# A mixture-of-experts kernel with seven-product block multiplication: preparation steps held back during one product, one subtraction moved to GpSimd

## The chip, the core and the metric

The kernel runs on one core of one Trainium2 chip. The metric is the device time of one execution, in microseconds (us). In the texts below the engines have the names of the profile: PE is TensorE (matrix multiplication), DVE is VectorE, ACT is ScalarE, POOL is GpSimd, SP is SyncE, which issues the transfers.

## What is computed

Three layers follow each other, all in float32: an attention over short windows, a layer of four experts, and a feed-forward layer.

```python
# attention: 2 x 8 heads, 768 positions of 64; chunks of 32 see 16 to the left, 8 to the right and 8 memory keys
scores = scale * np.matmul(q_c, k_full.transpose(0, 1, 3, 2))
a = np.exp(scores - np.max(scores, axis=-1, keepdims=True)); a = a / (a.sum(-1, keepdims=True) + 1e-9)
out[:, :, c_start:c_end] = np.matmul(a, v_full)
# experts: x is 1536 x 512, four of them, hidden size 1024
p = domain_probs / (domain_probs.sum(-1, keepdims=True) + 1e-09)
for e in range(4):
    out += p[:, e:e + 1] * (np.maximum(x @ w1[e], 0.0) @ w2[e])
# feed-forward: hidden size 2048
h = x @ w_in
g = np.maximum(h, 0.0) + alpha * np.minimum(h, 0.0)
return g @ w_out
```

The weights of the last layer arrive as 64-bit floats and are turned into 32-bit ones on the chip.

## The kernel before, in words

**Tiling.** The hidden units of both layers are cut into 24 pairs of blocks, numbered p: 16 for the experts (p = 0 to 15) and 8 for the feed-forward layer (p = 16 to 23). The 1536 tokens are folded into 768 columns, and a tile is one p with 384 of these columns (c0 = 0 or 384). For a tile, `gemm1` (L654) multiplies the first weights by the tokens and applies the activation, and `gemm2` (or `gemm2_two`, `gemm2_rows`) multiplies the result by the second weights. PE's order is written out by hand in `order`: `gemm1` of a tile, then `gemm2` of the tile before. Around the change of layers two tiles are taken together: `gemm1` of p = 14 and 15 with the same columns and then one double `gemm2` for both, and the same for p = 16 and 17.

**Seven products.** `gemm1` computes a 2 x 2 block product with seven multiplications in place of eight: a, b, d, a again, c, d again, c again, in this order. The second parts of a, d and c accumulate on top of what is in the bank. Between the products DVE and ACT form sums: `add("c", t, q["b"])` (L738, in the trace `b<-c,t`) reads bank c after its first part, and the second part of c may start only when this reading is done. Its cover is the second part of d, six matmuls.

**Three passes.** Each float32 operand is split into a high part, a cast to the format that PE takes (ACT), and a low part, the rest (POOL or DVE). A product is high x high, high x low and low x high. So the activation leaves a `gg` tile in two steps of `high()` (L700): ACT's cast, then POOL's subtraction. `gemm2` needs both: for each block its third matmul reads POOL's low part.

**Preparation streams.** What prepares later work is written as generators: `w` (weights: combinations `s`, high parts `wh`, low parts `wl`), `c` (conversion of the 64-bit weights) and, between the layers, `x0` and `x384` (`transition`, which runs `prep_x` on three blocks of 128 columns each). Each `yield` gives the time at which the next step is due. The planner keeps a clock `now`, which moves by 0.013 + n/2400 us for each matmul of n columns, so by 0.173 us for 384. `product` (L647) is called for each matmul; before it traces the matmul, it traces every step that is due: `att_poll`, `begin`, `lag_poll` (activations) and `prep_poll` (the streams). Each engine then executes its instructions in exactly this program order (`keep_in_program_order`); semaphores alone tie the engines together. So what the planner decides is the order on each engine, not the time.

**prep_x (L164).** For a block of tokens it forms differences in a tile `st` of three slices. The pool of `st` has one buffer, which all blocks share. The order is: DVE writes slices 0, 1 and 2; then for z = 0 ACT casts slices 0 and 1 into `xh`, and DVE writes their low part into `xl` (L190); then DVE overwrites slice 1 with `b21 - st[:, 1]` (L184); then for z = 1 ACT casts slices 1 and 2, and DVE writes their low part. POOL writes the low parts of the plain tokens (L178, L188). The steps of `x0` are 1.1 us apart, those of `x384` 0.88 us.

**Names in the trace.** The helper that records instructions hides their lines (nearly all have L61), so the rows are read by tiles: `y` is a bank of `gemm2`, `st`, `xh`, `xl` belong to `prep_x`, `g` and `gg` to the activation, `wl` and `wh` to the weights, `u` and `t` to the sums.

Of the kernel before, what the change touches and what calls it, by code (L numbers as in the profile page):

```python
# [10 lines left out]
F32 = mybir.dt.float32  # L11
# [55 lines left out]
def tile_kernel(ctx: ExitStack, tc: tile.TileContext, qk, v, wa, wq, dpt, alpha, out):  # L67
    nc = tc.nc
    scale = 1.0 / float(D) ** 0.5
    pe_, dve, act, pool, sync = (Pinned(tc, e) for e in (nc.tensor, nc.vector, nc.scalar, nc.gpsimd, nc.sync))  # L70
# [71 lines left out]
    xh = xp.tile([P, 14, NCOL], F32R, name="xh")  # L142
    xl = xp.tile([P, 14, NCOL], F32R, name="xl")
# [5 lines left out]
    def acc_of(cs):  # L149
        h, c = divmod(cs.start, half)  # L150
        return acc[:, h, :, :, c:c + cs.stop - cs.start]
# [12 lines left out]
    def prep_x(c0, n):  # L164
        cs = slice(c0, c0 + n)
        here = acc_of(cs)
        b11, b12, b21, b22 = here[:, 0:2, 0], here[:, 0:2, 1], here[:, 2:4, 0], here[:, 2:4, 1]

        st = bp.tile([P, 3, 2, n], F32, tag="st", name=f"st{c0}")
        sub = ALU.subtract  # L170
        act.copy(xh[:, 0:4, cs], here[:, :, 0])
        dve.tensor_tensor(out=st[:, 0], in0=b12, in1=b11, op=sub)
        yield
        dve.tensor_tensor(out=st[:, 1], in0=b22, in1=st[:, 0], op=sub)
        act.copy(xh[:, 4:6, cs], b22)
        yield
        dve.tensor_tensor(out=st[:, 2], in0=b22, in1=b12, op=sub)
        pool.tensor_tensor(out=xl[:, 0:4, cs], in0=here[:, :, 0], in1=xh[:, 0:4, cs].bitcast(F32), op=sub)  # L178
        yield
        for z in (0, 1):  # L180
            r = slice(6 + 4 * z, 10 + 4 * z)
            t_ = st[:, z:z + 2].rearrange("p a b n -> p (a b) n")
            if z == 1:
                dve.tensor_tensor(out=st[:, 1], in0=b21, in1=st[:, 1], op=sub)  # L184
                yield
            act.copy(xh[:, r, cs], t_)
            if z == 0:
                pool.tensor_tensor(out=xl[:, 4:6, cs], in0=b22, in1=xh[:, 4:6, cs].bitcast(F32), op=sub)  # L188
            yield
            dve.tensor_tensor(out=xl[:, r, cs], in0=t_, in1=xh[:, r, cs].bitcast(F32), op=sub)  # L190
            yield

    def transition(c0, n):
# [149 lines left out]
    def att_poll(force=False):  # L343

        while True:
            due = [x for x in att["live"] if x[0] <= now[0] and clear(x[2])]
            room = att["next"] < NU and len(att["live"]) < LIVE and clear(att["next"])
            if due:
                x = due[0]
                try:  # L350
                    att["stage"][x[2]] += 1
                    lat = next(x[1])
                    x[0] = now[0] + lat
                except StopIteration:
                    att["live"].remove(x)
                    att["over"].add(x[2])
                    while att["done"] in att["over"]:
                        att["done"] += 1
            elif room and att["start"] <= now[0]:
                g = unit(att["next"])  # L360
                att["start"] = now[0] + (PACE0 if force else PACE)
                att["next"] += 1
                x = [0.0, g, att["next"] - 1]
                att["live"].append(x)
                x[0] = next(g) + now[0]
                att["stage"][x[2]] = 1
            elif force:
                times = [x[0] for x in att["live"] if clear(x[2])]
                if room:
                    times.append(att["start"])  # L370
                now[0] = max(now[0], min(times))
                continue
            else:
                return
            if force:
                return
# [228 lines left out]
    def step(name):  # L605
        x = streams[name]
        if x[1] is not None and not x[1]():
            return False
        try:
            x[0], x[1] = next(x[2])  # L610
        except StopIteration:
            del streams[name]
        return True

    def prep_poll():
        for name in list(streams):
            while name in streams and streams[name][0] <= now[0] and step(name):
                pass
# [15 lines left out]

    glist = []
    lag = []
    hold = [False]

    def later(t, f):
        lag.append((now[0] + t, f))  # L640
        lag.sort(key=lambda x: x[0])
# [5 lines left out]
    def product(*a, n, **kw):  # L647
        att_poll()
        begin()
        lag_poll()  # L650
        prep_poll()
        mm(*a, n=n, **kw)

    def gemm1(p, c0, n, parity, last):  # L654
        cs = slice(c0, c0 + n)
        nm = f"{p}_{c0}"
        q = {}

        def prod(z, a, b, start, stop):
            if start:  # L660
                q[z] = bank(f"{z}{nm}")[:, :n]
            prep_force("w", lambda: (p, a) in w1)
            while p == 0 and b >= T4 and att["x"] < -(-(c0 + n) // BLK):
                att_poll(force=True)
            wh, wl = w1[p, a]
            k = 0
            for kd in range(2):
                f = slice(kd * P, (kd + 1) * P)
                for w_, x_ in ((wh, xh), (wh, xl), (wl, xh)):
                    product(q[z], w_[:, f], x_[:, 2 * b + kd, cs], n=n,  # L670
                            start=start and k == 0, stop=stop and k == 5, skip_group_check=True)
                    k += 1
            if last:
                used1.add((p, USE.index(a)))

        def add(z, other, out):
            dve.tensor_tensor(out=out, in0=q[z], in1=other, op=ALU.add)

        def tmp(name):
            return bp.tile([P, 384], F32, tag=name, name=f"{name}{nm}")[:, :n]  # L680

        gs = {}

        def gelu(blk, src):

            i, ab = divmod(blk, 2)

            lag_poll(lambda: len(glist) < 2 or glist[-2][1] in glist[-2][0])
            glist.append((gs, blk))
            if p >= NP1 and i == 0:  # L690
                if ab == 0:
                    g2 = bp.tile([P, 2, 384], F32, tag="pb", bufs=2, name=f"g2_{nm}")
                    gs["g2"] = g2
                g = gs["g2"][:, ab, :n]
            else:
                g = bp.tile([P, 384], F32, tag="g", bufs=4, name=f"g{blk}_{nm}")[:, :n]
            gg = bp.tile([P, 2, 384], F32R, tag="gg" + "AB"[parity], bufs=4, name=f"gg{blk}_{nm}")
            gh, gl = gg[:, 0, :n], gg[:, 1, :n]

            def high():  # L700
                act.copy(gh, g)
                pool.tensor_tensor(out=gl, in0=g, in1=gh.bitcast(F32), op=ALU.subtract)
                gs[blk] = (gh, gl)

            def whole():
                dve.scalar_tensor_tensor(out=g, in0=src, scalar=0.0, in1=g,
                                         op0=ALU.max, op1=ALU.add)
                later(0.8, high)

            if p < NP1:  # L710
                pb = pb_t[2 * p * P // F1, c0, n]
                dve.scalar_tensor_tensor(out=g, in0=src, scalar=0.0, in1=pb[:, ab, :n],
                                         op0=ALU.max, op1=ALU.mult)
                later(0.7, high)
            else:
                fi = 2 * (p - NP1) + i

                def negative():
                    act.activation(g, src, AF.Relu, scale=-1.0)
                    act.mul(g, g, nalpha[:, fi:fi + 1])  # L720
                    later(1.4, whole)

                later(0.0, negative)

        hold[0] = p >= NP1
        prod("a", A11, B11, True, False)
        u2 = tmp("u2")
        act.copy(u2, q["a"])
        hold[0] = False
        prod("b", S2, T2, True, True)  # L730
        add("b", u2, u2)
        prod("d", S1, T1, True, False)
        t = tmp("t")
        add("d", u2, t)
        prod("a", A12, B21, False, True)
        gelu(0, q["a"])
        prod("c", S3, T3, True, False)
        add("c", t, q["b"])  # L738
        prod("d", S4, B22, False, True)
        gelu(3, q["b"])  # L740
        add("d", u2, q["d"])
        prod("c", A22, T4, False, True)
        gelu(1, q["d"])
        add("c", u2, q["c"])
        gelu(2, q["c"])
        return gs
# [187 lines left out]
    def begin():  # L934
        while begun and att["next"] >= begun[0][0]:
            begun.pop(0)[1]()

    for i, (what, k, *other) in enumerate(order):
        p, c0, n = tiles[k]
# [141 lines left out]
```

## Time and profile before

| what | value |
|---|---|
| time, median of 3 runs (lowest to highest) | 818.88 us (818.68 to 819.94) |
| time of the profiled execution | 816.98 us |
| its span from first to last instruction | 815.2 us |
| PE busy | 800.1 us, 98% of the span |
| DVE, POOL, ACT busy | 578.6, 563.2 and 330.8 us |

The span is the time from the first instruction to the last; 1.8 us of the profiled execution lie around it. The profiled execution is 1.9 us shorter than the median. Busy shares are means over the whole span; what a stage is bound by is read from the waits and from the engines' instructions in order of time.

### The profile page before, as it was taken

What the parts mean: (1) busy time and instruction counts of PE and PEld (TensorE: products, weight loads), DVE (VectorE), ACT (ScalarE), POOL (GpSimd) and SP (SyncE); (2) the same over time, 40 slices, a digit from 0 to 9 for tenths busy, and PEclk for the clock granted to TensorE, in tenths of its full rate; (3) what the DMA queues carried; (4) which work ended last, traced back from release to release, by engine and by line L of the source; (5) the groups of instructions that cost most, each with busy time, mean ns of one, the idle gap of its engine ahead of it and who ended that gap; (6) DMA issues with size and microseconds to landing.
All of it is one profiled execution on the core that took longest, in us unless ns stands there. A gap on an engine that the chain in (4) does not pass through costs nothing.

```text
span 815.2 us, 14396 instructions
## 1 busy us (share of the span) xinstructions
PE 800.1 (98%) x5439; PEld 763.3 (94%) x5439; DVE 578.6 (71%) x1087; ACT 330.8 (41%) x718; POOL 563.2 (69%) x587
## 2 busy tenths in 40 slices
PE   7989999999999999999999999999999999999998
PEld 5778999999999999999999999999798998998996
DVE  4777477867867877867877767587964877756555
ACT  3656524133223223323322323154762666555441
POOL 2867777777887877977787872293954987867511
PEclk9999999999999999999999999999999999999999
DMA  8792121332231332313422302001002132211003
GB/s 258 232 293 88 52 91 39 113 122 64 94 104 63 115 116 68 103 68 90 117 92 90 117 27 78 26 27 53 27 14 101 41 118 89 80 40 51 1 1 154
DMA packets 29781, 71.66 MB, mean 88 GB/s; under 512 B 4624, under 2 KB 7696, under 8 KB 29712
## 3 DMA queue, kind: packets, MB, share of 16 engines
q1 hardware_dynamic: 29712, 70.75, 26.3%
q8 instruction: 42, 0.69, 0.3%
q14 instruction: 27, 0.22, 0.1%
HBM read 59.18 MB, written 11.56 MB: 87 GB/s over the span
## 4 chain that ended last, share of the span: by engine, by line
PE 91%; DVE 3%; ACT 2%; DMA 2%; issue 1%; POOL 1%; SPq 0%; DVEq 0%; POOLq 0%; ACTq 0%
PE y L61 49%; PE a L61 12%; PE c L61 12%; PE d L61 11%; PE b L61 6%; DMA raw<-in_wa 1%; DMA qk<-in_qk 1%; PE x L61 1%; PE two L61 1%; DVE pe L61 1%; PE wps0.0_84 L61 0%; DVE mx L61 0%; SPq L61 0%; ACT pe L61 0%; ACT g L61 0%
## 5 line engine op out<-in xcount | busy, mean ns | idle before, releaser
L61 POOL TENSOR_TENSOR gg<-g,gg 128x384 fp32r<-128x384 f32 x192 | 202.2, 1064 | 118.9 <-ACT gg L61 116.9
L61 PE MATMUL y<-gg,wh 128*128 128x384 f32 x1024 | 265.1, 334 | 0.4 <-POOL gg L61 0.2
L61 DVE TENSOR_TENSOR acc<-y,acc 128x384 f32<-128x384 f32 (+1 forms) x296 | 170.1, 584 | 70.9 <-PE y L61 69.3
L61 PEld LDWEIGHTS y<-gg,wh 128*128 128x128 f32 x1024 | 185.1, 188 | 1.1 <-POOL gg L61 0.5
L61 PE MATMUL y<-gg,wl 128*128 128x384 f32 x512 | 171.1, 334 | 0.0
L61 ACT CAST gg<-g 128x384 fp32r<-128x384 f32 x192 | 97.6, 512 | 151.9 <-DVE g L61 151.5
L61 POOL TENSOR_TENSOR wl<-raw,wh 128x256 fp32r<-128x256 f32 (+1 forms) x112 | 114.1, 1027 | 44.5 <-ACT wh L61 28.7
L61 PE MATMUL y<-wh,gg 128*128 128x512 f32 x384 | 120.7, 390 | 0.0
L61 ACT COPY u<-a 128x384 f32<-128x384 f32 x48 | 23.0, 479 | 197.8 <-PE a L61 197.8
L61 PEld LDWEIGHTS y<-gg,wl 128*128 128x128 f32 x512 | 96.1, 188 | 0.0
L61 PEld LDWEIGHTS y<-wh,gg 128*128 128x128 f32 x384 | 72.0, 188 | 15.0 <-POOL gg L61 0.3
L61 PE MATMUL y<-wl,gg 128*128 128x512 f32 x192 | 74.9, 390 | 0.0
L61 POOL TENSOR_TENSOR wl<-s,wh 128x256 fp32r<-128x256 f32 x88 | 68.2, 782 | 4.4 <-ACT wh L61 4.1
L61 DVE TENSOR_TENSOR u<-b,u 128x384 f32<-128x384 f32 x48 | 26.8, 557 | 60.2 <-PE b L61 55.0
L61 POOL TENSOR_TENSOR fl<-fl,fm 128x512 f32<-128x512 f32 x32 | 41.3, 1292 | 32.8 <-DVE fm L61 20.7
L61 PE MATMUL a<-xh,wh 128*128 128x384 f32 x184 | 61.7, 335 | 0.0
L61 PE MATMUL a<-xh,wl 128*128 128x384 f32 x184 | 61.6, 335 | 0.0
L61 PE MATMUL d<-xh,wl 128*128 128x384 f32 x184 | 61.6, 335 | 0.0
L61 PE MATMUL d<-xl,wh 128*128 128x384 f32 x184 | 61.6, 335 | 0.0
L61 PE MATMUL a<-xl,wh 128*128 128x384 f32 x184 | 61.6, 335 | 0.0
L61 ACT CAST wh<-raw 128x256 fp32r<-128x256 f32 (+1 forms) x116 | 54.7, 492 | 16.8 <-PE y L61 14.2
L61 PE MATMUL d<-xh,wh 128*128 128x384 f32 x184 | 61.5, 334 | 0.0
(121 smaller groups left out, 1573.1 us busy)
## 6 DMA issues: line engine op xcount, KB each, us to landing
fr<-in_wq SPq DMA_DIRECT2D x32, 512.0 KB, 3.8
raw<-in_wa SPq DMA_DIRECT2D x28, 512.0 KB, 3.9
w2s<-fl SPq DMA_DIRECT2D x32, 256.0 KB, 2.4
raw<-w2s SPq DMA_DIRECT2D x16, 512.0 KB, 3.6
qk<-in_qk SPq DMA_DIRECT2D x24, 312.0 KB, 4.7
v<-in_v SPq DMA_DIRECT2D x48, 130.0 KB, 3.8
out<-acc SPq DMA_DIRECT2D x12, 256.0 KB, 2.0
pb<-p_dram SPq DMA_DIRECT2D x6, 384.0 KB, 3.5
```

The lines of the kernel that those rows point to most:

```text
L61: return self.tc.keep_in_program_order(f(*a, **kw))
```

## The change

While the first part of product c of a tile with p > 0 is traced (six matmuls), `prep_poll` is not called. Steps of the streams that come due in this time are traced at the first matmul of the next product, after `add("c", t, q["b"])`. Activations (`lag_poll`) go on as before. Apart from this, in `prep_x` the low part of the differences with z = 0 is computed by POOL; the one with z = 1 stays on DVE.

```diff
-            dve.tensor_tensor(out=xl[:, r, cs], in0=t_, in1=xh[:, r, cs].bitcast(F32), op=sub)
+            (dve if z else pool).tensor_tensor(out=xl[:, r, cs], in0=t_, in1=xh[:, r, cs].bitcast(F32), op=sub)
...
-    hold = [False]
+    hold, quiet = [False], [False]
...
         lag_poll()
-        prep_poll()
+        if not quiet[0]:
+            prep_poll()
         mm(*a, n=n, **kw)
...
         gelu(0, q["a"])
+        quiet[0] = p > 0
         prod("c", S3, T3, True, False)
+        quiet[0] = False
         add("c", t, q["b"])
```

## Rows read from the trace of the kernel before

**Rows 1.** The page, first part: busy time, share, instructions of each engine.

```profile
PE 800.1 (98%) x5439; PEld 763.3 (94%) x5439; DVE 578.6 (71%) x1087; ACT 330.8 (41%) x718; POOL 563.2 (69%) x587
```

**Rows 2.** Waits of PE after 70 us: who waited for whom, total, times, longest.

```profile
PE c L61 <- DVE b L61: 1.8, 2, 1.4
PE y L61 <- POOL gg L61: 0.2, 1, 0.2
```

**Rows 3.** Two stretches: their length; PE, PEld, DVE, ACT, POOL busy; PE clock; transfers.

```profile
529.75:544.95 15.20, 14.88 (x85) 14.48 (x85) 13.14 (x25) 9.22 (x22) 13.04 (x13) 1.00 0.01 1
577.87:594.44 16.57, 16.57 (x74) 13.43 (x73) 16.26 (x23) 8.26 (x18) 16.49 (x15) 1.00 0.09 32
```

**Rows 4.** PE in order of time, where c's second part starts: start, duration, [idle before].

```profile
496.33 0.44 PE L61 MATMUL c<-xh,wh 128*128 128x384 f32 x1
...
543.12 0.34 PE L61 MATMUL d<-xh,w 128*128 128x384 f32 x1
543.79 0.44 PE L61 MATMUL c<-xh,w 128*128 128x384 f32 x1 [0.33 <-DVE b L61]
...
574.95 0.34 PE L61 MATMUL d<-xh,w 128*128 128x384 f32 x1
576.71 0.45 PE L61 MATMUL c<-xh,w 128*128 128x384 f32 x1 [1.43 <-DVE b L61]
```

**Rows 5.** DVE in order of time ahead of the last two of these.

```profile
543.18 0.55 DVE L61 TENSOR_TENSOR b<-c,t 128x384 f32<-128x384 f32 x1
...
574.79 1.39 DVE L61 TENSOR_TENSOR xl<-st,xh 128x512 fp32r<-128x512 f32 x1 [1.07 <-ACT xh L61]
576.10 0.55 DVE L61 TENSOR_TENSOR b<-c,t 128x384 f32<-128x384 f32 x1
576.57 0.75 DVE L61 TENSOR_TENSOR st<-acc,st 128x256 f32<-128x256 f32 x1
```

**Rows 6.** POOL in order of time, tiles of p = 14 and 15.

```profile
531.91 0.74 POOL L61 TENSOR_TENSOR wl<-raw,wh 128x256 fp32r<-128x256 f32 x1 [14.15 <-ACT wh L61]
...
549.04 1.45 POOL L61 TENSOR_TENSOR gg<-g,gg 128x384 fp32r<-128x384 f32 x1
```

**Rows 7.** PE in the double `gemm2` of p = 14 and 15.

```profile
551.02 0.51 PE L61 MATMUL y<-gg,wh 128*128 128x384 f32 x2
```

**Rows 8.** POOL in order of time, tiles of p = 16 and 17.

```profile
561.28 1.29 POOL L61 TENSOR_TENSOR wl<-raw,wh 128x512 fp32r<-128x512 f32 x1 [7.32 <-ACT wh L61]
...
573.38 1.02 POOL L61 TENSOR_TENSOR gg<-g,gg 128x384 fp32r<-128x384 f32 x1 [1.39 <-ACT gg L61]
...
575.59 1.45 POOL L61 TENSOR_TENSOR gg<-g,gg 128x384 fp32r<-128x384 f32 x1
...
577.88 3.05 POOL L61 TENSOR_TENSOR wl<-raw,wh 128x512 fp32r<-128x512 f32 x2
...
583.31 1.20 POOL L61 TENSOR_TENSOR gg<-g,gg 128x384 fp32r<-128x384 f32 x1
```

**Rows 9.** PE in the double `gemm2` of p = 16 and 17.

```profile
584.25 0.39 PE L61 MATMUL y<-wl,gg 128*128 128x512 f32 x1
584.56 0.73 PE L61 MATMUL y<-wh,gg 128*128 128x512 f32 x2
```

**Rows 10.** Groups by form, 529 to 600 us: count, busy us, mean ns, idle before.

```profile
L61 POOL TENSOR_TENSOR gg<-g,gg 128x384 fp32r<-128x384 f32 x16 | 19.4, 1228 | 5.9 <-ACT gg L61 5.9
L61 POOL TENSOR_TENSOR xl<-acc,xh 128x512 fp32r<-128x512 f32 x6 | 8.6, 1429 | 0.0
L61 DVE TENSOR_TENSOR xl<-st,xh 128x512 fp32r<-128x512 f32 x12 | 11.1, 928 | 1.9 <-ACT xh L61 1.8
```

**Rows 11.** Groups of the whole kernel, the same columns.

```profile
L61 POOL TENSOR_TENSOR gg<-g,gg 128x384 fp32r<-128x384 f32 x192 | 202.2, 1064 | 118.9 <-ACT gg L61 116.9 <-PE y L61 1.1
```

**Rows 12.** ACT in order of time behind the stall at 576.71.

```profile
578.24 0.62 ACT L61 CAST xh<-st 128x512 fp32r<-128x512 f32 x1
...
579.27 0.62 ACT L61 ACTIVATE g<-g,nalpha 128x384 f32<-128x384 f32 x1
```

## The prediction

> **What bounds the kernel now.** The page's first part is read first: PE works 98% of the span [rows 1], so only the moments in which PE waits, or will wait, can change the time. Next come PE's waits behind the attention, after 70 us. There are two kinds, 2.0 us together [rows 2]: PE before the second part of c, waiting for DVE's sum `b<-c,t`, and PE in `gemm2`, waiting for POOL's low part of `gg`. All lie where the layers change (p = 14 to 17). PE in order of time gives their full price, from start to start: a matmul of 384 columns follows the one before after 0.17 us, and the first one after a wait takes 0.44 in place of 0.34, 0.1 more. The second part of c should start at 543.12 + 0.17 = 543.29 and starts at 543.79; at the other place it should start at 575.12 and starts at 576.71 [rows 4]. With the slow restarts that is 0.6 + 1.7 us. The one at 496.33 has the same long duration [rows 4], so a short wait too, too short for the list; I take 0.2 for it. Together 2.5 us.
>
> DVE in order of time shows the cause at the third place: `xl<-st` stands ahead of `b<-c,t`. It waited 1.07 us for its ACT cast and then took 1.39, so `b<-c,t` ran at 576.10, with PE behind it [rows 5]. At the second place DVE's queue is full and a `st` step traced in c lies ahead of the sum at 543.18 [rows 5]. So the change aims at real waits.
>
> But POOL must be read too. From 531.91 to past 550 and from 573.38 on its instructions follow each other without a gap: in the rows behind these no idle time is printed [rows 6, 8]. It is busy 13.04 of 15.20 us in the one stretch (nearly all of it after its first instruction), 16.49 of 16.57 in the other [rows 3]. PE needs what stands at the end of this queue.
>
> **The change, part by part.** *The hold.* For tiles with p > 0 the steps of up to six matmuls (1.04 us) move behind the sum. In the steady stretch PE never waits for the sum [rows 2], so nothing is gained there; the steps that move are weights and conversion, used a tile later, hidden by ten weight slots. Their transfers on SP (raw weights, next chunk) move by at most that 1.04 us, with nothing but preparation behind them. I put this at 0. If the cover failed, a weight would be traced by force ahead of its product and PE would wait for one cast and one subtraction, about 1.5 us each time. At 496, 543 and 576 the sum gets its place: up to 2.5 us gained.
>
> *The subtraction.* Six instructions of 128x512 leave DVE (three for each half of the columns) and go to POOL. On DVE they average 0.93 us; POOL's instructions of the same shape here average 1.43, and the shortest full-width one in these rows took 1.29 [rows 8, 10]. DVE gets lighter by 6 x 0.93 = 5.6 us, POOL heavier by 6 x 1.29 to 1.43 = 7.7 to 8.6 us, in the two stretches where it is full.
>
> *The added wait.* The tile `st` has one buffer. The next instruction on it, DVE's `st<-acc,st` for z = 1 (at 576.57 for block 3 [rows 5]), overwrites slice 1, which POOL now still has to read. On one engine program order settled this; now DVE stops until POOL, deep in its queue, has come to the subtraction. Behind it on DVE stand the sums and activations of the tile, behind those ACT's casts of `gg`, behind those POOL again.
>
> *What this costs at p = 14 and 15.* In program order the subtraction of block 0 comes right behind the first `gg` of p = 14. That of block 1 comes behind the second `gg` of p = 15, ahead of its third: counting the planner's 1.1 us steps, with the hold, puts it about half a microsecond before that one. So the third `gg`, ended at 549.04 + 1.45 = 550.49 [rows 6], gets two more instructions ahead of it: +2.6 to +2.9. Some comes back, because POOL runs slower beside DVE: `gg` averages 1.23 us here against 1.06 in the whole kernel [rows 10, 11]. Two subtractions fewer on DVE give back 0 to 0.6; I take 0.5. The new end is 550.49 + 2.75 - 0.5 = 552.7 (between 552.5 and 553.4 at the ends, or 551.9 if more comes back). PE reads it at 551.02 [rows 7]; this is the third matmul of the second block in the second tile. The old slack of 0.53 is gone, and PE is 552.7 - 551.02 = **1.7 us later than before** (0.9 to 2.4). The 0.6 gained at 543.79 is in this already: PE comes earlier and waits longer.
>
> *At p = 16 and 17.* POOL has time to recover in between (7.32 us idle before 561.28 [rows 8]). From 573.38 on its queue is again the limit: the third `gg` of p = 17 ends at 583.31 + 1.20 = 584.51, and the matmul that reads it, due at 584.25 + 0.227 = 584.48, starts at 584.56 [rows 8, 9]. There is no slack at all, even with PE held up at 576.71. So the 1.7 us gained there can't be kept; PE would wait at 584.5 in its place. What POOL gets on top decides. The subtraction of block 3 lands between the two `wl` of 577.88 [rows 8]. Without the DVE work that slowed `gg` at 575.59 to 1.45, the queue is 0.3 earlier: 577.6, then `wl` 1.3 and the subtraction 1.3, until 580.2. DVE has stood before `st<-acc,st` since about 577. Now: this instruction, the sum into c, the activation of block 3 and its ACT cast, some 0.5 each (DVE's sum took 0.55 [rows 5]): 582.2. ACT then takes its two steps on block 2, together some 1.1 (the second took 0.62), and the cast of `st`, 0.62 [rows 12]: 583.9. DVE takes the z = 1 subtraction, 0.7, and the activation of block 1, 0.55; ACT the cast, 0.5; POOL the third `gg`, 1.06 [rows 11]: 586.7. Before it was 584.51, so PE is **2.2 us later**. The lower bound is the queue alone, 1.29 - 0.3 = 1.0; the upper one is 3.1, with DVE's steps as long as its rows show under contention.
>
> *Blocks 4 and 5* go the same way, beside the rest of the double `gemm2`, where DVE is busy 16.26 of 16.57 us [rows 3]. The chain gives block 5's low part at about the time PE needs it in the next tile. I put it at 0, bounds 0 and +1.
>
> **Sum:** -0.2 (496.33) + 1.7 + 2.2 = +3.7; I take +3.4, since instructions on DVE start some 0.1 before the one ahead has ended (576.10 + 0.55 against 576.57 [rows 5]), four times in the chain. On the profiled execution that is 816.98 + 3.4 = 820.4. The median of the runs is 1.9 above that execution, so the prediction is 818.88 + 3.4 = **822.3 us**. The ends: -0.2 + 0.9 + 1.0 = +1.7 (820.6), and -0.2 + 2.4 + 3.1 = +5.3 (824.2).
>
> **A rule beside this.** By the rows, the moved instruction takes 1.43 / 0.93 = 1.5 times as long on POOL as on DVE [rows 10]; DVE's mean holds its own slow cases. The Trainium skill, GPSIMD Engine Reference, section 3.1 (Elementwise, side by side), gives GpSimd 1.96 times VectorE's time for an addition of two tensors and advises VectorE for such work. The trace agrees in direction and not in size. An estimate by that page would be 1.96 x 0.93 = 1.8 us for each, and the first place would cost 2.6 in place of 1.7.
>
> **The rivals.**
> - *The waits go and nothing takes their place.* DVE, relieved, runs ahead, POOL at its best rate takes the subtractions without delaying `gg`: -0.2 - 0.6 - 1.7 - 0.2 = -2.7, so 816.2. For it speak PE's waits, which are all on DVE but one. Against it speaks the matmul at 584.56, which is already late for POOL. It would need POOL 1.3 us faster over some ten instructions. Chance 0.09.
> - *Only one place pays.* The third `gg` of p = 15 is in time (slack 0.53, contention gone) and only p = 17 loses: -0.2 - 0.6 + 2.2 = +1.4; or the other way round, -0.2 + 1.7 - 1.9 = -0.4. So 818.5 to 820.3. Chance 0.15.
> - *The change hardly alters the order* where it matters, and the time stays near 818.9. Against it: `xl<-st` of 574.79 is itself traced during c and changes its engine. Chance 0.03.
> - *The forecast*, PE waits for `gg` in both double `gemm2`: 820.6 to 824.2. It decides as soon as POOL's third `gg` is over 0.53 us later at the first place, and at once at the second. Chance 0.73.
>
> **How the numbers follow.** About 0.2%, 1.6 us, is what a measurement of this kernel can tell from no change. The forecast is slower by more than that (0.73); the second and third rival lie within it (0.18); the first is faster (0.09). The range takes in the forecast with its bounds down to 819.6, so half of the second rival, and up to 824.0.
>
> **What the profile after would show.** Right: PE's waits for `b<-c,t` are gone; PE's waits for POOL's `gg` have grown from 0.2 to some 2 to 4 us, at about 551 and 583; DVE idles before `st<-acc,st` until POOL's `xl<-st` ends; POOL has no gap from 532 to past 555. Wrong: POOL's `gg` of p = 15 ending before 551, no DVE idle time ahead of `st<-acc,st` (the wait would not be there), or a PE wait in tiles of p below 14, which would mean that the held steps are not free.

## The result, and the profile after

| | before | after |
|---|---|---|
| median of 6 runs each (lowest to highest) | 817.66 us (816.16 to 819.94) | 822.59 us (820.65 to 824.97) |
| ratio after / before, 95% interval | | 1.0065 [1.0047, 1.0082] |
| profiled execution, and its span | 816.98, 815.2 us | 824.97, 823.2 us |

The kernel is slower, as forecast, and the median lies 0.3 us from the predicted 822.3. That is luck in part. With three more runs the kernel before has a median of 817.66, not 818.88. The difference is 0.0065 x 817.7 = 5.3 us (3.8 to 6.7), and I had forecast 3.4. The direction and the main mechanism held; the sum was too small. Two signs that I had named did not show. PE's waits for POOL's `gg` were to grow from 0.2 to 2 to 4 us, and they stayed at 0.2, because PE met other waits first. And POOL was to have no gap from 532 to past 555, but it stands idle for 0.54 us before 546.89.

Repeated executions of one kernel differ by several us, because the attention ahead takes a different time (the tile p = 14 with c0 = 384 starts between 528.8 and 533.0 us in the twelve profiles), so stretches are compared here more than whole times. Each stretch comes from one profiled execution; that of the changed kernel is the slowest of its six, 2.4 us above their median. Of the 8.0 us between the two spans, 2.1 lie ahead of p = 14 with c0 = 0. In the 26 tiles of the steady stretch, from `gemm1` of p = 1 to that of p = 14 with c0 = 0, PE takes 405.60 us in both kernels (84.42 to 490.02 before, 86.53 to 492.13 after): in this pair the hold costs nothing there and brings nothing. From there to p = 14 with c0 = 384 it is 39.52 us where it was 39.73: the 0.2 of the wait at 496.33 [rows 4].

The first part of the page shows where the instructions went: six of DVE's are POOL's now (compare [rows 1]).

```profile
PE 804.5 (98%) x5439; PEld 766.2 (93%) x5439; DVE 581.7 (71%) x1081; ACT 330.3 (40%) x718; POOL 574.4 (70%) x593
```

DVE has six instructions fewer and is yet busy 3.1 us longer; POOL has six more and is busy 11.2 us longer, of which the six account for some 7.7 (six of 1.28 us, shown further down).

PE's waits of the changed kernel after 70 us (who waited for whom, total, times, longest) answer [rows 2]:

```profile
PE y L61 <- POOL wl L61: 1.9, 1, 1.9
PE y L61 <- ACT gg L61: 1.1, 2, 0.8
PE a L61 <- ACT u L61: 1.0, 1, 1.0
PE y L61 <- POOL gg L61: 0.2, 1, 0.2
```

The waits for `b<-c,t` are gone from the list, as intended (0.3 us of the one at p = 15 are left, too short for it). In their place PE waits for three other things. DVE's waits between 490 and 610 us have the new line that the prediction was built on:

```profile
DVE st L61 <- POOL xl L61: 10.6, 5, 3.1
```

DVE stands 10.6 us in five waits, up to 3.1 us, before it may overwrite slice 1 of `st`.

**The first place (p = 15, c0 = 384).** All engines of the changed kernel in order of time, the lines that hang on each other:

```profile
538.35 1.30 POOL L61 TENSOR_TENSOR xl<-st,xh 128x512 fp32r<-128x512 f32 x1
...
539.68 0.94 DVE L61 TENSOR_TENSOR st<-acc,st 128x256 f32<-128x256 f32 x1 [0.94 <-POOL xl L61]
...
540.66 0.62 ACT L61 CAST xh<-st 128x512 fp32r<-128x512 f32 x1 [1.83 <-DVE st L61]
...
542.66 0.47 ACT L61 COPY u<-a 128x384 f32<-128x384 f32 x1
...
543.19 0.44 PE L61 MATMUL a<-xh,w 128*128 128x384 f32 x1 [0.97 <-ACT u L61]
...
552.72 2.16 POOL L61 TENSOR_TENSOR gg<-g,gg 128x384 fp32r<-128x384 f32 x2
...
553.96 0.51 PE L61 MATMUL y<-gg,wh 128*128 128x384 f32 x2
```

POOL's low part ends at 539.65, DVE overwrites the slice, ACT casts it, and only then ACT comes, two `gg` casts later, to the copy `u<-a` that frees bank a for its second part. This second part was due at 542.05, 1.14 us earlier, and restarts slowly, 0.1 more. With two short stalls behind it (0.1 before d at 545.39, 0.3 before c at 546.74) this stretch holds 1.7 us of stalls where the kernel before had 0.6, so PE is 1.04 later. The first of POOL's two `gg` from 552.72 (2.16 together), the third of p = 15, ends at some 553.7, and PE comes to read it at 553.96: just in time, because PE is late already. Counted from the start of A1, the first of the stretches listed below, this `gg` ends 1.3 us later than before.

**The second place (p = 17, double `gemm2` from 579.10).** Again all engines in order of time:

```profile
580.22 1.29 POOL L61 TENSOR_TENSOR wl<-raw,wh 128x512 fp32r<-128x512 f32 x1
...
581.47 1.29 POOL L61 TENSOR_TENSOR xl<-st,xh 128x512 fp32r<-128x512 f32 x1
582.72 1.01 POOL L61 TENSOR_TENSOR gg<-g,gg 128x384 fp32r<-128x384 f32 x1
582.79 1.22 DVE L61 TENSOR_TENSOR st<-acc,st 128x256 f32<-128x256 f32 x1 [2.99 <-POOL xl L61]
...
584.98 0.51 ACT L61 CAST gg<-g 128x384 fp32r<-128x384 f32 x1 [3.25 <-DVE g L61]
...
585.54 0.50 PE L61 MATMUL y<-wh,gg 128*128 128x512 f32 x1 [0.80 <-ACT gg L61]
585.63 1.00 POOL L61 TENSOR_TENSOR gg<-g,gg 128x384 fp32r<-128x384 f32 x1 [1.90 <-ACT gg L61]
...
586.59 1.27 POOL L61 TENSOR_TENSOR wl<-raw,wh 128x512 fp32r<-128x512 f32 x1
...
587.91 0.79 PE L61 MATMUL y<-wl,gg 128*128 128x512 f32 x1 [1.87 <-POOL wl L61]
...
589.47 0.79 PE L61 MATMUL y<-wh,gg 128*128 128x512 f32 x1 [0.34 <-ACT gg L61]
589.49 2.19 POOL L61 TENSOR_TENSOR gg<-g,gg 128x384 fp32r<-128x384 f32 x2 [1.64 <-ACT gg L61]
590.59 1.22 PE L61 MATMUL y<-wh,gg 128*128 128x512 f32 x2
...
592.03 1.06 PE L61 MATMUL y<-wh,gg 128*128 128x512 f32 x2
592.89 0.63 PE L61 MATMUL y<-wl,gg 128*128 128x512 f32 x1
```

DVE idles 2.99 us, so ACT idles 3.25 before the second `gg`, so POOL idles 1.90 before its low part, and the second `wl` of the weights stands behind that in POOL's order. In [rows 8] the two `wl` followed each other directly. PE waits three times within five microseconds. At 590.59 it reads the third `gg` of p = 17, which POOL has just finished (at 590.53).

And then something that the kernel before does not show at this place: stretches of the changed kernel (length; PE, PEld, DVE, ACT, POOL busy; granted clock; transfers):

```profile
579.10:588.00 8.90, 6.23 (x27) 4.59 (x26) 3.79 (x6) 5.10 (x11) 6.86 (x7) 0.99 0.00 1
588.00:595.00 7.00, 6.66 (x15) 4.41 (x16) 3.93 (x6) 1.91 (x4) 5.51 (x5) 0.52 0.23 75
```

Behind the waits the granted clock is 0.52 for seven microseconds, in the main the lower level of 1.2 GHz, and matmuls of 512 columns follow each other every 0.43 us (592.03, two of them, then 592.89, in the rows above) in place of 0.227. PE counts as busy and does half the work: 7.00 x 0.48 = 3.4 us of clock are lost, a small part of it while PE stood anyway.

**Stretch by stretch.** PE's starts in order of time give the lengths below, for the runs of the next section too: `gemm1` of p = 14 and 15 with c0 = 384 (A1), the double `gemm2` behind it (Ay), the same two of p = 16 and 17 with c0 = 0 (B1, By), and `gemm1` with c0 = 384 (C).

| kernel | A1 | Ay | B1 | By | C | sum | against before |
|---|---|---|---|---|---|---|---|
| before | 15.20 | 16.65 | 16.27 | 16.57 | 14.58 | 79.27 | |
| after | 16.24 | 16.64 | 14.57 | 23.29 | 14.59 | 85.33 | +6.06 |
| e1 hold alone | 15.90 | 16.64 | 14.56 | 17.89 | 14.59 | 79.58 | +0.31 |
| e2 POOL alone | 16.55 | 16.64 | 14.56 | 22.45 | 14.59 | 84.79 | +5.52 |
| e3 both, no wait on `st` | 15.66 | 17.52 | 14.56 | 18.58 | 14.58 | 80.90 | +1.63 |
| e4 both, weights not held | 16.29 | 16.64 | 14.56 | 22.20 | 14.58 | 84.27 | +5.00 |
| e5 both, POOL for blocks 0 to 2 | 16.25 | 16.68 | 14.55 | 18.85 | 14.59 | 80.92 | +1.65 |
| e6 both, POOL for blocks 3 to 5 | 15.91 | 16.65 | 14.56 | 22.78 | 14.58 | 84.48 | +5.21 |
| e7 both, PE's wait filled | 16.27 | 16.65 | 14.56 | 21.44 | 15.39 | 84.31 | +5.04 |
| e8 POOL alone, no wait on `st` | 15.98 | 17.09 | 14.56 | 20.37 | 14.58 | 82.58 | +3.31 |
| e9 hold for p = 17, other order of `gemm2` | 15.21 | 16.64 | 14.56 | 16.36 | 15.11 | 77.88 | -1.39 |
| e10 both, other order of `gemm2` | 16.27 | 16.64 | 14.56 | 18.69 | 17.69 | 83.85 | +4.58 |

Without any stall A1 is 14.56 and By 16.33 (72 matmuls at 0.2268). So the change takes 1.7 from B1 and gives 1.0 to A1 and 6.7 to By.

### The profile page after: what moved, and what is told of

It is laid out like the page before. It is cut to its first block, busy times and chain, and to the rows that moved or that the text cites. A ratio compares the mean times of both kernels' runs of the same rounds, so it can differ in the third digit from the quotient of the medians.

```text
span 823.2 us, 14401 instructions
## 1 busy us (share of the span) xinstructions
PE 804.5 (98%) x5439; PEld 766.2 (93%) x5439; DVE 581.7 (71%) x1081; ACT 330.3 (40%) x718; POOL 574.4 (70%) x593
## 4 chain that ended last, share of the span: by engine, by line
PE 90%; ACT 3%; DVE 3%; POOL 2%; DMA 2%; issue 1%; SPq 0%; POOLq 0%; DVEq 0%; ACTq 0%
PE y L61 48%; PE a L61 12%; PE c L61 11%; PE d L61 11%; PE b L61 6%; DMA raw<-in_wa 1%; POOL xl L61 1%; DMA qk<-in_qk 1%; DVE pe L61 1%; PE two L61 1%; POOL gg L61 1%; DVE mx L61 1%; ACT g L61 1%; PE x L61 0%; ACT xh L61 0%
## 5 line engine op out<-in xcount | busy, mean ns | idle before, releaser
L61 DVE TENSOR_TENSOR acc<-y,acc 128x384 f32<-128x384 f32 (+1 forms) x296 | 167.5, 582 | 47.8 <-PE y L61 46.4
L61 POOL TENSOR_TENSOR wl<-raw,wh 128x256 fp32r<-128x256 f32 (+1 forms) x112 | 117.0, 1051 | 45.1 <-ACT wh L61 29.3
L61 PE MATMUL y<-wh,gg 128*128 128x512 f32 x384 | 123.3, 396 | 1.1 <-ACT gg L61 1.1
L61 POOL TENSOR_TENSOR wl<-s,wh 128x256 fp32r<-128x256 f32 x88 | 70.4, 804 | 6.4 <-ACT wh L61 6.2
L61 ACT CAST wh<-raw 128x256 fp32r<-128x256 f32 (+1 forms) x116 | 54.7, 492 | 15.1 <-PE y L61 11.4
```

What stands on the lines that cost most here:

```text
L61: return self.tc.keep_in_program_order(f(*a, **kw))
```

## The experiments

**e1: the hold alone.** Both low parts stay on DVE.

```diff
-            (dve if z else pool).tensor_tensor(out=xl[:, r, cs], ...
+            dve.tensor_tensor(out=xl[:, r, cs], ...
```

> The hold alone; all subtractions of prep_x stay on VectorE. Theory (the loss comes from GpSimd's longer queue and from VectorE's new wait for it): neither is there, so no loss. The sum gets its place at 496, 543 and 576 (2.5 us), but at p = 16 and 17 TensorE still needs the third gg, which ends at 584.5 as before, so only 0.8 us of the 2.5 stay: 0.5 to 1.0 us faster than before. No idle time of VectorE in front of st. Rival (the held weight steps cause the loss by themselves, because the low part of the second weights of p = 17 comes behind two gg): 1 to 4 us slower than before, with TensorE waiting for wl in the double gemm2 of p = 16 and 17.

Measured: 817.97 against 818.22 us, ratio 0.9997 [0.9978, 1.0015]; +0.31 us over the stretches. PE's waits after 70 us in this kernel:

```profile
PE y L61 <- POOL wl L61: 1.0, 1, 1.0
PE a L61 <- ACT u L61: 0.6, 1, 0.6
```

The whole time can't tell my forecast from no change (its interval reaches from 1.8 us faster to 1.2 slower); the stretches show no gain, and the wait for `wl` that the rival named is there, without its loss. The waits for `b<-c,t` are gone from this list too, some 2 us, and yet nothing is gained in the end. At p = 15 PE waits 0.6 for `u` in place of 0.3 for the sum, and A1 is 0.7 longer. DVE's rows show where that begins, first before, then in e1:

```profile
534.65 0.73 DVE L61 TENSOR_TENSOR xl<-st,xh 128x512 fp32r<-128x512 f32 x1
535.30 0.55 DVE L61 TENSOR_TENSOR b<-c,t 128x384 f32<-128x384 f32 x1
```

```profile
534.18 0.57 DVE L61 TENSOR_TENSOR b<-c,t 128x384 f32<-128x384 f32 x1 [0.41 <-PE c L61]
534.65 1.42 DVE L61 TENSOR_TENSOR xl<-st,xh 128x512 fp32r<-128x512 f32 x1
```

Held back, DVE's `xl<-st` stands behind the sum and takes 1.42 in place of 0.73 us there; counted from the start of A1, the copy `u` comes 0.9 us later than before. At p = 17 POOL's order, here in e1, shows what PE waits for:

```profile
577.75 1.29 POOL L61 TENSOR_TENSOR wl<-raw,wh 128x512 fp32r<-128x512 f32 x1
579.00 1.99 POOL L61 TENSOR_TENSOR gg<-g,gg 128x384 fp32r<-128x384 f32 x2
580.95 1.72 POOL L61 TENSOR_TENSOR wl<-raw,wh 128x512 fp32r<-128x512 f32 x1
582.63 2.36 POOL L61 TENSOR_TENSOR gg<-g,gg 128x384 fp32r<-128x384 f32 x2
```

The two `wl` that stood together in [rows 8] now have two `gg` between them. The hold moved the weight stream, and PE waits 1.0 us for the second `wl`. But that wait only stands ahead of the next one: the third `gg`, the first of the two from 582.63, ends at 583.83, and PE reads it at 583.88, 0.1 after it was due. Counted from the start of B1 that is 0.4 us earlier than before, and no more of the 1.7 could be kept. So near the change of layers the hold costs 0.7 us at p = 15, by a step of the tokens, and gains 0.4 at p = 17.

**e2: the subtraction alone.** The kernel before with `(dve if z else pool)`, no hold.

> The subtraction for z = 0 on GpSimd, without the hold. Theory: the new wait of VectorE and the longer queue of GpSimd are both there, so it is slower than before by 2 to 4 us; TensorE waits for the copy u (p = 15) and for gg (p = 17), not for wl. Rival (held weights are the cause): within 1 us of before, or faster, since the 1.7 us wait at 576.7 goes.

Measured: 825.91 us, ratio 1.0090 [1.0073, 1.0106], so 7.4 us slower, far more than expected; +5.52 us over the stretches. DVE's wait on `st` and PE's waits in e2, two answers:

```profile
DVE st L61 <- POOL xl L61: 15.0, 5, 5.2
```

```profile
PE y L61 <- ACT gg L61: 3.2, 2, 2.6
PE a L61 <- ACT u L61: 1.3, 1, 1.3
PE y L61 <- POOL gg L61: 0.6, 2, 0.4
PE c L61 <- DVE b L61: 0.2, 1, 0.2
```

The subtraction on POOL carries the loss. It also takes the waits for `b<-c,t` at p = 15 and 17 away nearly alone: the instruction that stood ahead of the sum in [rows 5] is now on POOL. The 0.2 in the list lies elsewhere, at 436.89, in the steady stretch. That stretch takes 406.17 us here and 406.11 and 406.19 in e8 and e9, which have one such wait each; the eight profiles with a hold in every tile have none and take 405.60. So the hold can save some 0.5 us there, though the profile of the kernel before, with no hold, has no such wait either.

**e3: both, without the wait on `st`.** The tile gets a fourth slice, so that z = 1 writes a slice that nobody reads. The padding shrinks to make room.

```diff
-        st = bp.tile([P, 3, 2, n], F32, tag="st", name=f"st{c0}")
+        st = bp.tile([P, 4, 2, n], F32, tag="st", name=f"st{c0}")
...
-            t_ = st[:, z:z + 2].rearrange("p a b n -> p (a b) n")
+            t_ = st[:, 2 * z:2 * z + 2].rearrange("p a b n -> p (a b) n")
...
-                dve.tensor_tensor(out=st[:, 1], in0=b21, in1=st[:, 1], op=sub)
+                dve.tensor_tensor(out=st[:, 2], in0=b21, in1=st[:, 1], op=sub)
...
```

> The whole change, but st has four slices, so that VectorE's subtraction for z = 1 writes a slice that GpSimd does not read (the wait is taken away by taking away its cause; an unrelated small tile shrinks by 32 bytes to make room). Theory: VectorE's waits for GpSimd's xl (10.6 us of idle time) all but vanish, and with them the copy u's delay (1.3 us at p = 15) and the late activation of block 3: 3 to 5 us faster than the changed kernel, 0 to 2 us slower than before. Rival (GpSimd's load of 8 us more is the cause): within 1 us of the changed kernel.

Measured: 820.35 us, ratio 1.0029 [1.0019, 1.0039]; +1.63 over the stretches. DVE's 10.6 us of waiting on `st` shrink to 1.2. PE's waits in e3, and the one at 552.88 in order of time:

```profile
PE y L61 <- POOL wl L61: 1.7, 1, 1.7
PE y L61 <- POOL gg L61: 0.8, 2, 0.6
PE a L61 <- ACT u L61: 0.3, 1, 0.3
PE c L61 <- DVE b L61: 0.2, 1, 0.2
```

```profile
552.88 0.62 PE L61 MATMUL y<-gg,wh 128*128 128x384 f32 x2 [0.58 <-POOL gg L61]
```

The added wait accounts for 6.06 - 1.63 = 4.4 us of the stretches and for 1.0065 - 1.0029, about 2.9 us, of the whole time. Part of the 4.4 is the clock, which does not fall here. From the start of By to its matmul that reads the third `gg`, PE takes 8.68 us in e3 and 11.49 in the changed kernel: 2.8 us are the wait itself. The rest is POOL's load and the hold: the wait for POOL's `gg` of p = 15 that I had predicted for the changed kernel appears here (552.88), where DVE isn't held up, and `wl` is late at p = 17. The clock is 1.00 from 579 on, although PE stood 1.7 us once.

**e4: both, with the weights not held.** During the first part of c the stream `w` alone goes on.

```diff
...
-        if not quiet[0]:
-            prep_poll()
+        prep_poll("w" if quiet[0] else None)
```

> The whole change, but the weight stream is not held (tokens and conversion are). Theory: the second low part of the weights of p = 17 comes ahead of two gg in GpSimd's order again, TensorE no longer waits 1.9 us for it and keeps its clock; what is left is the wait for gg: 1.5 to 3.5 us faster than the changed kernel, 1.5 to 3.5 us slower than before. Rival (the wait for wl only stands in front of one for gg that is as long): within 1 us of the changed kernel.

Measured: 823.85 us, ratio 1.0069 [1.0047, 1.0090]; +5.00 over the stretches. In POOL's order the second `wl` (580.66) is back right behind the subtraction (579.41), and PE's wait for `wl` is gone. PE waits 3.2 us for `gg` instead (1.09, 0.42 and 1.64 at 583.78, 584.93 and 587.06, the middle one for POOL's step), and the clock falls all the same (0.56 from 587 to 590). So the rival's account holds: the order of `wl` decides which wait ends last, not how late PE is. It is worth 1.1 us over the stretches and nothing that the whole time shows. A1 stays at 16.29: what the hold costs there is not the weights.

**e5 and e6: the subtraction on POOL for half of the blocks.** `(dve if z or c0 >= NCOL // 2 else pool)` gives POOL blocks 0 to 2 alone (e5); `c0 < NCOL // 2` gives it blocks 3 to 5 alone (e6).

> The whole change, but the subtraction moves to GpSimd only for the first half of the columns (three instructions, beside p = 14 and 15). Theory: the new wait then costs only there, by the late copy u (some 1.3 us, of which hold and old wait are to be taken off); the stretch of p = 16 and 17 is as with the hold alone. 0 to 1.5 us slower than before. Rival (the loss comes from GpSimd's whole load, the same for each half): half of the changed kernel's loss, 2.5 us.

> The whole change, but the subtraction moves to GpSimd only for the second half of the columns (three instructions, beside the double gemm2 of p = 16 and 17). Theory: nearly all of the changed kernel's loss is here, 4 to 5.5 us slower than before, with VectorE waiting for GpSimd before st and TensorE waiting in the double gemm2 and then running at the lower of its two clocks. Rival: half of the loss, 2.5 us.

Measured: e5 820.58 us, 1.0040 [1.0021, 1.0058], +1.65 over the stretches; e6 824.39 us, 1.0093 [1.0075, 1.0111], +5.21. By the stretches the loss sits at p = 16 and 17: blocks 3 to 5 cost most of it. By the whole time both runs lost more than expected, e5 3.3 and e6 7.6 us, together twice the 5.3 of the changed kernel; the runs do not show why. By the stretches e6 lost what I had forecast, and e5 a little more. In e5 the clock is 1.00 throughout the two stages; in e6 it is 0.50 from 590 to 593.

At p = 16 and 17 the program of e5 is that of e1, and yet By is 18.85 in place of 17.89. DVE's `st<-acc,st` and `xl<-st` there took 1.00 and 1.83 us in e5 (579.40, 583.46), and 0.41 and 0.97 in e1 (576.77, 580.57). So the moment at which DVE and POOL meet can move a stretch by 1 us, and smaller differences between single profiles prove little.

**e7: both, with PE's wait filled.** 18 matmuls of 512 columns into a spare bank that nobody reads, ahead of the second block's products in the double `gemm2` of p = 16 and 17.

```diff
+                if m == 1 and c0 == 0:
+                    o = bank("idle")
+                    for _ in range(18):
+                        pe_.matmul(o..., xh[:, 0, 0:P], xh[:, 0:2, 0:256], start=True, stop=True)
```

> The whole change; between the two tiles of the first double gemm2 of p = 16 and 17 stand 18 extra matmuls of 512 columns (4.1 us at the full clock) whose result nobody reads, so that TensorE works in the time in which it would wait. Theory: the work that TensorE waits for is not earlier or later, but the granted clock stays at its upper level, and the stretch behind the wait no longer takes 0.427 us for a matmul in place of 0.227: 1.5 to 3 us faster than the changed kernel. Rival (the clock fell for another reason, or the time behind the wait is hidden by work that is late anyway): not faster than the changed kernel, or up to 1 us slower.

Measured: 824.57 us, ratio 1.0089 [1.0059, 1.0119]; +5.04 over the stretches, with By 21.44 in place of 23.29, of which the next tile gives 0.8 back. Its clock in the stretch in which the changed kernel had 0.65 and 0.50:

```profile
587.00:590.00 3.00, 3.00 (x14) 2.27 (x13) 2.25 (x4) 1.61 (x4) 1.57 (x2) 1.00 0.11 20
590.00:593.00 3.00, 2.58 (x10) 1.72 (x10) 2.67 (x4) 1.53 (x4) 2.78 (x3) 1.00 0.46 154
```

With PE kept busy the clock stays at 1.00, and work that nobody needs makes this stretch 1.85 us shorter. PE reads the third `gg` 11.55 us after the start of By, as late as in the changed kernel (11.49), so the 1.85 come behind it. The whole time doesn't show them (the interval reaches from 1.0059 to 1.0119, and the median is not below that of the changed kernel), so the forecast of 1.5 to 3 us was missed and this isn't a remedy. One profile of each speaks for the fall being a consequence of the waits.

**e8: the subtraction on POOL, without hold and without the wait on `st`.** e2 with the edit of e3.

> The subtraction on GpSimd with st in four slices (no wait of VectorE for GpSimd), without the hold: GpSimd's load alone. Theory: GpSimd's queue ahead of the third gg is 1.3 us longer at p = 17 and 2.6 us at p = 15, and no weight step is late: 1 to 2.5 us slower than before, PE waiting for gg. Rival (the load costs nothing, the loss is the wait alone): within 0.5 us of before, or faster.

Measured: 820.31 us, ratio 1.0043 [1.0021, 1.0065], 3.5 us slower (1.7 to 5.3), more than the middle of what I expected; +3.31 over the stretches. PE waits for POOL's `gg` (2.2 us, four times), 0.6 for `b<-c,t` and 0.5 for `u`. POOL's load alone delays the third `gg` at both places; the term was real, but in the changed kernel other waits come ahead of it. By holds a fall of the clock too (0.62 from 590 to 593), e3's does not, so the 1.7 us between e8 and e3 can't be put down to the hold. Between e2 and e8 the wait on `st` is priced without the hold: 2.2 us over the stretches, with a fall of the clock in both, and PE reads the third `gg` 11.57 and 8.87 us after the start of By, 2.7 apart, as between the changed kernel and e3.

**e9: the hold for p = 17 alone, and another order of the double `gemm2`.** Both subtractions on DVE, as in e1. In addition p = 16 takes six of its blocks before p = 17 comes, not four, so the third `gg` of p = 17 is needed later. The edit against e1:

```diff
-        quiet[0] = p > 0
+        quiet[0] = p == NP1 + 1
...
-                for b in blocks[:4]:
+                for b in blocks[:6]:
...
-            for b in blocks[4:]:
+            for b in blocks[6:]:
```

> A try at a version faster than both: all subtractions on VectorE, the hold only in the tiles of p = 17, and the double gemm2 of p = 16 and 17 runs all six blocks of p = 16 ahead of those of p = 17 (four before), so that the third gg is needed 2.7 us later. Theory: the 1.7 us wait at the second part of c goes and is not given back at gg, since gg is now early; p = 14 and 15 stay as before: 1.0 to 2.0 us faster than before, TensorE's waits of the stretch from the first tile of p = 14 on fall from 2.0 to 0.4 us. Rival (the next wait stands right behind, for a bank or for the tokens of the next tile): within 0.5 us of before.

Measured: 816.25 against 818.26 us, ratio 0.9976 [0.9963, 0.9990]; -1.39 over the stretches. PE's waits in e9:

```profile
PE c L61 <- DVE b L61: 0.5, 2, 0.3
PE b L61 <- DVE xl L61: 0.2, 1, 0.2
PE y L61 <- POOL gg L61: 0.2, 1, 0.2
```

B1 is 14.56 and By 16.36: the 1.7 us won at c are kept, and 0.5 is given back in C. As forecast, it is faster than both kernels, if only by 0.24% against the one before. With e1, where PE reads the third `gg` as soon as it is there, it bears out the reading of [rows 9]: this `gg`, not the sum, was the limit behind the stall at 576.71. Of the 0.5 for `b<-c,t`, 0.3 lies at p = 15 as before and 0.2 in the steady stretch, which has no hold here.

**e10: both parts of the change, with e9's order of `gemm2`.**

> The whole change, with the same order of six blocks. Theory: what TensorE waits for in the double gemm2 of p = 16 and 17 is 2.7 us further away, so of the 7 us that this stretch is too long 4 to 5 go, the fall of the clock among them: 3 to 5 us faster than the changed kernel, 0.5 to 2.5 us slower than before. Rival (VectorE, which runs late there, then holds back the banks or the next tile's tokens): 0 to 2 us faster than the changed kernel.

Measured: 821.87 us, ratio 1.0051 [1.0031, 1.0072]; +4.58 over the stretches. By the ratios that is 1.1 us faster than the changed kernel, by the stretches 1.5: the rival's case. By falls from 23.29 to 18.69, with the clock at 1.00, and C rises from 14.59 to 17.69. In e10 PE waits in the next tile:

```profile
PE b L61 <- POOL xl L61: 1.0, 1, 1.0
...
PE b L61 <- ACT xh L61: 0.7, 1, 0.7
```

The conversion of the tokens itself is now late. As long as DVE waits for POOL, time saved in `gemm2` is lost in the tile that reads the tokens.

## Why the prediction was right, and where its sum was not

**Right: the waits for `b<-c,t` go and the tile `st` brings a larger one.** The waits of after show both. e3 prices the added wait, 4.4 us over the stretches, the clock included; e2 shows that it needs no hold, and e2 against e8 that it costs 2.2 without one.

**Right: the 1.7 us at p = 17 can't be kept, because POOL's third `gg` is the limit.** e1 loses all but 0.4 of them again and e9, which needs this `gg` later, keeps them.

**Wrong size, first place: 1.0 in place of 1.7 us, by another wait.** I followed POOL's queue to the third `gg` of p = 15 and left out ACT's copy `u`, which stands behind the cast that waits for DVE. PE stops some 10 us earlier than I said, and then `gg` is in time. This `gg` itself was 1.3 us later, where I had 2.2, so with a slack of 0.53 it alone would have cost 0.8. That 1.0 lies within my bounds is luck. The copy is not late by the wait for POOL alone: the hold by itself delays it by 0.9 of its 1.3 us (e1), and the subtraction without the hold makes PE wait for it as well (e2, 1.3). e3, with DVE free, shows the wait that I had worked out: Ay is 0.9 us longer than before.

**Wrong: the hold at 0.** It is free in the steady stretch (405.60 in both). But I had counted only weights and conversion among the steps that move. At p = 14 and 15 those of the tokens move too, and e1 loses 0.7 us in A1 by them; e4, which lets the weights go on, loses as much there as the changed kernel. At p = 17 the weight stream moves by up to 1.04 us, POOL meets the second `wl` two `gg` later, and PE waits for it (e1 1.0, after 1.9). I had the two `wl` together, as in [rows 8]. This wait stands in front of one for `gg`, so e4, without it, is hardly faster. The net price is small, +0.3 in e1, but in e1 it eats what the hold should bring.

**Mis-sized: the second place.** I had put the third `gg` of p = 17 at 586.7 in the time of the kernel before. Taken from the start of the double `gemm2`, it ends 589.49 + 1.04 - 579.10 = 11.4 us behind it, where the kernel before had 584.51 - 577.87 = 6.6. This start is 1.7 earlier, so `gg` is 3.1 us later, where I had 2.2. DVE's `st` took 1.22 and its `xl` 1.34 us beside POOL's subtractions; I had used 0.5 and 0.7. Both overruns together are 1.4 us, more than the 0.9 by which I was short, since POOL's own subtraction ended 0.4 earlier than I had put it.

**Missing: the fall of the clock.** By is 6.96 us longer than its 16.33 without a stall. 3.45 of that are the three waits with their restarts, and some 3 are matmuls at the lower level. Not all of the 3 count, since up to 590.59 PE would have stood for the third `gg` anyway: from there to the end of By it takes 11.80 us, and 9.89 in e7 at the full clock. So the fall costs 1.9 us, and the second place is 3.1 + 1.9 = 5.0 us, the 6.7 of By less the 1.7 of B1. No term of my sum had it, and no row of these stages of before could have given its size. But a fall as long as this isn't in every execution: the mean granted clock of the six runs of after is 0.992 to 0.998, and the two with 0.997 and 0.998 have at most 2.9 and 2.1 us of lost clock in the whole span, with the rounding, less than this stretch alone lost. A shorter fall can be in them, and the mean does not say where the clock fell: the kernel before has one in its attention (0.91 from 40 to 60 us). These two took 822.05 and 822.49 us, more than 4 us above the median of the kernel before, so it is slower without a fall of this length too. How much of the median's difference the fall makes is open, since the attention's scatter of some 2 us either way lies over it.

**Blocks 4 and 5: 0 was right in the changed kernel** (C 14.59), where PE comes late. e10, where PE comes 4.6 us earlier, shows that they are next.

**The price of the subtraction.** The groups between 529 and 600 us of the changed kernel (count, busy us, mean ns, idle before) answer [rows 10]:

```profile
L61 POOL TENSOR_TENSOR gg<-g,gg 128x384 fp32r<-128x384 f32 x16 | 17.3, 1088 | 8.8 <-ACT gg L61 8.8
L61 POOL TENSOR_TENSOR xl<-st,xh 128x512 fp32r<-128x512 f32 x5 | 6.4, 1284 | 1.0 <-PE y L61 1.0
L61 DVE TENSOR_TENSOR xl<-st,xh 128x512 fp32r<-128x512 f32 x5 | 4.1, 822 | 2.8 <-ACT xh L61 2.8
```

POOL takes 1.28 us, the lower of my two values, and `gg` falls from 1.23 to 1.09: the relief was real. DVE's standing still isn't needed for it: in e3, where DVE hardly waits for POOL, `gg` averages 1.11, but there POOL's subtraction takes 1.41, near the upper of my values. The instruction that stayed on DVE takes 0.82, and 0.68 where POOL's doesn't slow it (542.07). 1.28 / 0.68 = 1.9. The Trainium skill, GPSIMD Engine Reference, section 3.1, gives 1.96. So the page had the ratio of undisturbed instructions right; the mean behind my 1.5 held DVE's slow cases beside POOL. The sum by that page, 2.6 at the first place, would still have been wrong, because the duration was not what decided.

**The rivals.** "Nothing takes the waits' place" fell with the list of waits. "Only one place pays" comes nearest to what happened among them: the first place lost 1.0 in A1, less than expected, and the second most of the rest (e6). "Hardly alters the order" fell with POOL's and DVE's rows.

## What to carry to other kernels

Before an instruction moves to another engine, list who next overwrites what it reads: in a tile with one buffer, program order on one engine becomes a wait between two, and here it made PE 2.7 to 2.8 us later at p = 17, where the load that was moved cost 0.7 (8.68 in e3 against 8.00 us in e1, from the start of By to the third `gg`). A stall that is removed is worth only the slack of the next thing the same engine reads; look for the matmul that starts exactly when its operand is ready, and loosen that first, as e9 does. Follow the chain behind a new wait through every engine's queue in order, copies that free a bank included, since the first thing to be late need not be the one that was nearly late before.

## What the runs showed of the hardware

- **Short waits can cost PE its clock.** In the changed kernel PE was busy 6.23 of 8.90 us, with waits of 0.80 and 1.87 us at the end of it, and then had a granted clock of 0.52 for 7 us. e2, e4, e6 and e8, with 1.8 to 3.9 us of PE's waits in the same stage, fell as well (0.50 to 0.67 in the lowest of the stretches of 3 us that were read). The kernel before (one wait of 1.43), e3 (one of 1.66), e5 (three, 1.6 together) and e10 (three, 1.5 together) stayed at 1.00, and so did e7, where the waits were filled. What decides is open: e8 fell with one wait of 1.60 and one of 0.19, and e3 with its 1.66 did not. The Trainium skill, TensorE: Matmul & The Clock Gate, Part 1, has the clock gated to half by how busy the engine has lately been. The trace agrees in the level: 0.50, and 0.43 us for 512 columns.
- **DVE and POOL slow each other both ways.** `st<-acc,st` takes 0.41 us undisturbed and 1.22 beside POOL's `gg` (582.79), `xl<-st` 0.68 and 1.34 (587.07). POOL's `gg` takes 1.01 undisturbed (582.72) and 1.45 in the slow case of the kernel before [rows 8]. An instruction of DVE that POOL's end releases starts just as POOL starts its next one, so it is likely to get the slow case: of the five `st<-acc,st` that waited for POOL four took 0.94 to 1.22 us, and the fifth, 0.43, came where POOL stood idle (595.05).
